# Top-k attention feeding a leaky-ReLU MLP on one core: eight small MLP chunks at the start instead of two, other units hurried, and eight units scored ahead instead of twelve

## The chip, the cores and the metric

The kernel runs on one core of one Trainium2 chip. The metric is the device time of one launch in microseconds (us). The kernel before takes 1465.96 us, the median of 3 runs (1465.23 to 1466.16). Work is done by five engines that run side by side: TensorE (PE in the profile, its weight loads PEld), VectorE (DVE), ScalarE (ACT), GpSimd (POOL) and SyncE (SP), which here issues the DMAs.

## The reference

Everything is float32 at the inputs and the output. There are 8 batches, 8 heads, 576 positions and a head width of 64.

```python
scores = scale * np.matmul(q, k.transpose(0, 1, 3, 2))
kth = np.partition(scores, -top_k, axis=-1)[..., -top_k:-top_k + 1]      # top_k = 32
scores = np.where(scores >= kth, scores, -1000000000.0)
scores = scores - np.max(scores, axis=-1, keepdims=True)
attn = np.exp(scores)
attn = attn / (np.sum(attn, axis=-1, keepdims=True) + 1e-09)
attn_out = np.matmul(attn, v)
x = attn_out.transpose(0, 2, 1, 3).reshape(4608, 512)
h = x @ w_in                          # 512 x 2048
out = np.maximum(0.01 * h, h) @ w_out # 2048 x 512
```

## The kernel before

**Units and steps.** The attention is cut into 144 units, one for each step of the main loop (line 609). A unit is 128 query rows of one pair of heads (or 64 rows of two pairs, where 576 isn't a multiple of 128). Four units in a row, one for each pair of heads, complete 128 tokens of the MLP's input `x`. A unit passes through the loop as `cur`, `old` and `older`: in step s, DVE finds the 32 largest scores of unit s (`top_k`, lines 289 to 306), POOL masks unit s-1 (lines 314 and 315), ACT takes its exponentials (line 318), and unit s-2 is normalised (lines 327 and 330) and transposed. The scores of two units are made on PE two steps ahead (`scores`, line 225), and copied out of PSUM by ACT (line 232).

**Transposing.** As a rule ACT splits the weights of a unit into 16-bit halves (line 339), SP writes them to DRAM (line 340), and a transposing DMA brings them back as `wT` (line 344). For units named in `HASTY` PE transposes them itself (`transpose_in_haste`, line 354, nine transposes), and ACT copies them to `wT` (line 360).

**Values.** `values_at(n)` says in which step, and where in it, PE multiplies a unit's weights with the values (`weigh_values`, line 381, two units at a time). Units below `UNHURRIED` (14) go to the middle of the step (n | 1) + 4, later ones to the end of the step (n | 1) + 3, and those in `HURRIED` one step sooner. ACT then copies the result to `x` (line 395).

**The MLP.** `CHUNKS` cuts the 4608 tokens into 2 chunks of 128 and 17 of 256. A chunk becomes ready when its last unit's values are in. A chunk of 256 tokens runs `w_in` as the stationary operand and `x` as the moving one (line 437), ACT applies the leaky ReLU (line 443), and PE multiplies with `w_out` (line 449). The first `EARLY` (2) chunks take another way, `hidden_of_few`: `x` is stationary, `w_in` moves 512 columns at a time (line 405), ACT applies the leaky ReLU into the tile `scale` (line 410), and PE transposes the result back (`turned`, line 421), which ACT copies to `gT` (line 422). In PSUM the tiles `ph`, `pt` and `pz` share the two buffers of the tag `ml`.

**The order on PE.** All engines run their instructions in the order in which the loop emits them. `mlp_steps(budget)` emits MLP work seven times in a step (`SLOTS`) until the budget, counted in matmul columns, is used up. The budget is a constant `EARLY_SHARE` (500) until the first chunk of 256 tokens is due, and after that the backlog spread evenly over the steps to the next due chunk. By the kernel's own count a chunk of 128 tokens of the early kind costs 17,408 columns and a chunk of 256 tokens 32,768.

**Units scored ahead.** The scores of twelve units named by `KEPT` (24, 25, 32, 33; 40, 41, 48, 49; 56, 57, 64, 65) are made in steps 0 to 5, while PE has no MLP work (`keep_scores`, line 276; how many in each step is in `EARLY_SCORES`). ACT copies them to `gT`, which the MLP doesn't use yet (line 280), SP writes them to DRAM (line 282), and they are fetched by DMA three steps ahead of their unit (line 287).

**Ahead of the loop.** The weights arrive as 64-bit words and are rounded on chip (`round_weights`); queries and keys for the units scored ahead are loaded into `raw` tiles by `load_early` (line 253).

Of the kernel before, what the change touches and what calls it, by code (L numbers as in the profile page):

```python
# [20 lines left out]
def kernel(  # L21
# [29 lines left out]
    WCH = 1024  # L51
    LEFT = S % P
    assert D == 64 and S == 576 and HP == 4 and B % 2 == 0 and LEFT == 64
    CHUNKS = [128] * 2 + [256] * 17
    assert sum(CHUNKS) == B * S
    CHMAX = max(CHUNKS)
    LOADED, LOADED_V = 5, 5
# [119 lines left out]
    def load_v(pi):  # L177
        v_of[pi] = loads.tile([P, NKC, 2, D], F32, name="vt", bufs=LOADED_V)
        nc.sync.dma_start(v_of[pi], vk[pi])
# [54 lines left out]
    def first_scores(u):  # L234

        ps = [ps_sc.tile([P, 2, 512], F32, name="wide", bufs=2) for i in range(2)]
        for half in range(2):
            for i, pi, side, r0 in u.parts:
                qt, kt = qk_of[pi]
                d = slice(side * D, (side + 1) * D)  # L240
                nc.tensor.matmul(ps[i][:, half, 0:HS], qt[d, u.q0:u.q0 + P],
                                 kt[d, half * HS:(half + 1) * HS], start=True, stop=True)
        yield
        u.both = work.tile([P, 2, S], F32, name="s_sb", bufs=5)
        u.s = [u.both[:, i, :] for i in range(2)]
        for i in range(2):
            nc.scalar.copy(u.s[i].rearrange("p (h n) -> p h n", h=2), ps[i][:, :, 0:HS])  # L247
# [109 lines left out]
    def keep_transposed(u):  # L357
        u.wT = work.tile([P, 2 * NKC - 1, P], F32, name="wT", bufs=3)
        for c0, c1, pt in u.parts_T:
            nc.scalar.copy(u.wT[:, c0:c1, :], pt[:, 0:c1 - c0, :])  # L360

    x_of = {}

    def x_at(token):

        c = 0
        while token >= CHUNKS[c]:
            token -= CHUNKS[c]  # L370
            c += 1
        return c, token
# [15 lines left out]
    def keep_values(u, po):  # L388
        n = u.rows
        po = po.rearrange("p (o n) -> p o n", n=n)  # L390
        ch, col = x_at(u.b * S + u.q0)
        if ch not in x_of:
            x_of[ch] = [xpool.tile([P, CHMAX], F32, name=f"x{c}") for c in range(HP)]
        for o, (pi, _, _) in enumerate(u.outs):
            nc.scalar.copy(x_of[ch][pi % HP][:, col:col + n], po[:, o, :])  # L395

    EARLY = 2

    def hidden_of_few(ch, x):

        g_of = {}
        for j in range(NFC // 4):
            ph = ps_ml.tile([P, 512], F32, name="ph", tag="ml")
            for c in range(HP):
                nc.tensor.matmul(ph, x[c][:, 0:P], w_in[c][:, j * 512:(j + 1) * 512],
                                 start=(c == 0), stop=(c == HP - 1))
                if c == 1:
                    yield 2 * 512
            g_of[j] = raws.tile([P, 2 * DMODEL], U16, name="scale", bufs=2).bitcast(F32)
            nc.scalar.activation(g_of[j], ph, AF.Prelu, alpha=SLOPE)  # L410
            yield 2 * 512
            if j:
                yield from turned(j - 1, g_of)
        few[ch] = g_of
# [3 lines left out]
    def turned(j, g_of):  # L418
        pt = ps_ml.tile([P, 4, P], F32, name="pt", tag="ml")
        for i in range(4):  # L420
            nc.tensor.transpose(pt[:, i, :], g_of[j][:, i * P:(i + 1) * P], ident)
        nc.scalar.copy(gT[:, 4 * j:4 * (j + 1), 0:P], pt)
        yield 2 * P

    def mlp(ch):

        n = CHUNKS[ch]
        t0 = sum(CHUNKS[:ch])
        x = x_of[ch]
        if ch < EARLY:  # L430
            yield from hidden_of_few(ch, x)
        for f0 in range(0, NFC if ch >= EARLY else 0, 2):
            ph = ps_ml.tile([P, 2, CHMAX], F32, name="ph", tag="ml")
            for i in range(2):
                f = f0 + i
                for c in range(HP):
                    nc.tensor.matmul(  # L437
                        ph[:, i, 0:n], w_in[c][:, f * P:(f + 1) * P], x[c][:, 0:n],
                        start=(c == 0), stop=(c == HP - 1),
                    )  # L440
                    if c == 1 or i == 0 and c == HP - 1:
                        yield 2 * max(n, 225)
            nc.scalar.activation(gT[:, f0:f0 + 2, 0:n], ph[:, :, 0:n], AF.Prelu, alpha=SLOPE)  # L443
            yield 2 * max(n, 225)
        for r0 in range(0, n, P):
            m = min(P, n - r0)
            pz = ps_ml.tile([P, 512], F32, name="pz", tag="ml")
            for f in range(NFC):
                nc.tensor.matmul(  # L449
                    pz[0:m, 0:DMODEL], gT[:, f, r0:r0 + m], w_out[f // 4][:, f % 4, :],  # L450
                    start=(f == 0), stop=(f == NFC - 1),
                )
                if f % 2 and f + 1 < NFC:
                    yield 2 * DMODEL
                if f == 7 and ch in few:
                    yield from turned(NFC // 4 - 1, few[ch])
            o_sb = work.tile([P, DMODEL], F32, name="o_sb", bufs=1)
            nc.scalar.copy(o_sb[0:m], pz[0:m, 0:DMODEL])  # L458
            nc.sync.dma_start(out[t0 + r0:t0 + r0 + m, :], o_sb[0:m])
            yield 2 * DMODEL  # L460

    def mlp_cost(ch):
        n = CHUNKS[ch]
        if ch < EARLY:
            return NFC * DMODEL + NFC // 4 * (HP * 512 + 2 * P)
# [21 lines left out]

    LAG = 3
    HURRY = 20
    HURRIED = (15, 23, 31)  # L490
    HASTY = (14, 15, 23, 31)
    UNHURRIED = 14
    MIDDLE, END = 0, 1

    def values_at(n):

        if n < UNHURRIED:
            return (n | 1) + LAG + 1, MIDDLE
        return (n | 1) + LAG - ((n | 1) in HURRIED), END

    steps = units

    KEPT = (24, 40, 56)
    EARLY_SCORES = {0: 4, 1: 2, 2: 1, 3: 2, 4: 1, 5: 2}

    def unit(n):
        return steps[n] if 0 <= n < len(steps) else None
# [2 lines left out]
    for n, u in enumerate(steps):  # L510
        ch, _ = x_at(u.b * S + u.q0)
# [11 lines left out]
    def slot_budget(s):  # L523

        after = [at for (at, _), _ in ready_at if at >= s]
        until = after[0] if after else s
        if len(after) >= len(CHUNKS) - EARLY:
            return EARLY_SHARE
        return backlog[0] / ((until + 1 - s) * SLOTS)

    EARLY_SHARE = 500
    SLOTS = 7

    with tc.manual_schedule():
        last = {p: n for n, u in enumerate(steps) for p in u.pairs}

        to_keep = [[steps[n] for n in (a, a + 1, a + 8, a + 9)] for a in KEPT]
        early_units = {u for us in to_keep for u in us}
        to_load, to_keep = list(to_keep), [u for us in to_keep for u in us]
# [27 lines left out]
        jobs = [round_weights(*job) for job in ROUNDED] if AS_WORDS else [iter(())] * len(ROUNDED)  # L567
        for n in range(len(jobs) + 1):
            if n == len(jobs) - 1:
                first = first_scores(steps[0])  # L570
                next(first, None)
            for job in jobs[max(n - 1, 0):n + 1][::-1]:
                next(job, None)
            if n == len(jobs) - 1:
                next(first, None)
                load_v(0)
                load_v(1)
            elif n == len(jobs):
                for _ in first_scores(steps[1]):
                    pass  # L580
            if n:
                load_weights(n + 2)
            if n >= len(jobs) - 2:
                load_early(to_load.pop(0))
            if 0 <= n - len(jobs) + HP + 1 < HP:
                load_qk(n - len(jobs) + HP + 1)

        def weights_of(u):
            reciprocals(u)
            normalize(u, 0)  # L590
            normalize(u, 1)
# [17 lines left out]
        for s in range(len(steps) + LAG + 1):  # L609
# [9 lines left out]

            at_first = s < HURRY and s - 2 in HURRIED  # L620
            if at_first:
                weights_of(older)
            slot()
            if old:
                mask(old, 0)
                mask(old, 1)
            late = s < HURRY and not {s - 1, s - 2} & set(HURRIED)
            if older and not late and not at_first:
                weights_of(older)
            mlp_steps(budget)  # L630
            weighed = values(s, MIDDLE)
            at_once = s - 2 in HASTY or any(at == (s, MIDDLE) for at, _ in ready_at)
            if at_once:
                keep(weighed, s, MIDDLE)
            slot()
            if older and late:
                weights_of(older)
            if s - 2 in HASTY:
                transpose_in_haste(older)
# [4 lines left out]
            if older:  # L644
                keep_transposed(older) if s - 2 in HASTY else transpose(older, lambda: mlp_steps(budget))
            if not older or s - 2 in HASTY:
                mlp_steps(budget)
# [18 lines left out]
            if new and s >= HURRY:  # L666
                scores(new)
            score_early(EARLY_SCORES.get(s, 0))
            budget = slot_budget(s + 1)
# [61 lines left out]
```

## Time and profile before

| | us |
|---|---|
| median of the runs (three) | 1465.96 |
| the profiled execution's own time | 1463.63 |
| its span, first to last instruction | 1461.7 |
| PE busy | 1405.5 |
| DVE busy | 1320.3 |
| ACT busy | 1100.9 |
| POOL busy | 1097.8 |
| step 0 begins on DVE | 61.4 |
| first MLP matmul on PE | 130.8 |
| step 43 begins on DVE | 449.2 |
| last `top_k` on DVE ends | 1375.7 |

All views are of the one profiled execution. A group row gives line, engine, operation, tiles, shapes and count, then the busy time in us and the mean duration in ns of one instruction, and after the second bar the idle time just ahead of these instructions and what ended it. A float32 matmul shows as two records, a transpose as one. Because matmuls overlap in the pipeline, the time that one record takes of PE is busy time divided by count, and not the mean duration. A row of the windows view gives a stretch of time, then the busy time of each engine in it, the granted clock of PE (1.00 is full) and the DMA share.

### The profile page before, as it was taken

To read this page: it belongs to the slowest core of one execution; us is meant where nothing else is said; L and a number is where in the kernel's file an instruction comes from. 1 tells how busy PE (TensorE), PEld (TensorE's weight loads), DVE (VectorE), ACT (ScalarE), POOL (GpSimd) and SP (SyncE) were. 2 spreads that over 40 slices of the span, in tenths; PEclk is the share of its full clock that TensorE was granted. 3 is DMA by queue.
4 is the path that set the end of the run, shared out by engine and by line. 5 is a ranking of instruction groups with operands and counts; after the bars stand their busy time and mean duration, and the time that the engine had idled before them with its cause. 6 is when DMAs were issued, how large, how long until landed. Compare 5 with 4: busy or idle time off the path is not lost.

```text
span 1461.7 us, 24213 instructions
## 1 busy us (share of the span) xinstructions
PE 1405.5 (96%) x8066; PEld 932.9 (64%) x8068; DVE 1320.3 (90%) x3401; ACT 1100.9 (75%) x1984; POOL 1097.8 (75%) x744
## 2 busy tenths in 40 slices
PE   7848999999989999999999999999999999999998
PEld 2425548576757676767676767676766666666674
DVE  7999999999999999999999999999999999999600
ACT  8878878677868777777778787777777777777710
POOL 3288888878888888888888787888887878787700
PEclk9968999999999999999999999999999999999999
DMA  8967543646576666676656655666566665554510
GB/s 320 344 219 225 140 119 101 194 128 181 151 192 179 172 167 188 156 194 169 157 163 170 169 138 141 171 164 166 149 156 171 164 151 143 153 141 130 150 43 14
DMA packets 394989, 239.03 MB, mean 164 GB/s; under 512 B 334576, under 2 KB 336112, under 8 KB 392944
## 3 DMA queue, kind: packets, MB, share of 16 engines
q1 hardware_dynamic: 394864, 237.48, 58.5%
q8 instruction: 63, 1.03, 0.3%
q14 instruction: 62, 0.51, 0.1%
HBM read 55.77 MB, written 99.09 MB: 106 GB/s over the span
## 4 chain that ended last, share of the span: by engine, by line
PE 77%; DVE 13%; ACT 4%; DMA 4%; issue 1%; SPq 0%; POOL 0%; DVEq 0%; ACTq 0%; POOLq 0%
PE pz L449 30%; PE ph L437 29%; PE wide L381 10%; DVE tops L301 5%; PE wide L225 5%; DVE pairs L304 4%; PE narrow L225 3%; DMA apart<-split 2%; ACT split L339 1%; DVE pairs L296 1%; DMA raw<-in_weights_dram 1%; ACT s_sb L318 1%; ACT s_sb L330 1%; DVE w_out L156 1%; DMA wT<-apart 1%
## 5 line engine op out<-in xcount | busy, mean ns | idle before, releaser
L314 POOL TENSOR_SCALAR pen<-s_sb,tops 128x576 f32<-128x576 f32 x288 | 638.3, 2216 | 203.8 <-DVE tops L301 135.6
L301 DVE MAX8 tops<-pairs 128x8 f32<-128x288 f32 (+1 forms) x1152 | 635.9, 591 | 0.0
L449 PE MATMUL pz<-w_out,gT 128*128 128x512 f32 x1152 | 505.1, 595 | 2.4 <-ACT scale L410 2.4
L437 PE MATMUL ph<-x,w_in 128*128 128x256 f32 x2176 | 482.6, 381 | 0.0
L304 DVE MATCH_REPLACE8 pairs<-tops,pairs 128x288 f32<-128x288 f32 (+1 forms) x864 | 460.1, 538 | 0.0
L437 PEld LDWEIGHTS ph<-x,w_in 128*128 128x128 f32 x2176 | 409.5, 190 | 75.5 <-issue 21.3
L315 POOL TENSOR_TENSOR s_sb<-s_sb,pen 128x576 f32<-128x576 f32 x288 | 406.9, 1413 | 24.0
L449 PEld LDWEIGHTS pz<-w_out,gT 128*128 128x128 f32 x1152 | 216.4, 190 | 266.2 <-issue 261.2
L339 ACT COPY split<-s_sb 128x1152 uint16<-128x1152 uint16 x280 | 309.5, 1146 | 1.7 <-DMA apart<-split 1.7
L330 ACT ACTIVATE s_sb<-s_sb,rz 128x576 f32<-128x576 f32 x288 | 207.7, 773 | 33.4 <-DVE rz L327 33.4
L318 ACT ACTIVATE s_sb<-s_sb,nbias 128x576 f32<-128x576 f32 x288 | 222.4, 772 | 6.4 <-POOL s_sb L315 6.4
L296 DVE TENSOR_TENSOR pairs<-s_sb 128x576 f32<-128x576 f32 x288 | 213.6, 780 | 9.5
L381 PEld LDWEIGHTS wide<-wT,vt 128*64 128x64 f32 x3200 | 161.2, 139 | 53.0 <-issue 36.2
L381 PE MATMUL wide<-wT,vt 128*64 128x128 f32 (+1 forms) x3200 | 179.0, 268 | 10.3 <-DMA wT<-apart 4.7
L443 ACT ACTIVATE gT<-ph 128x512 f32<-128x512 f32 x136 | 80.7, 593 | 58.6 <-PE ph L437 57.7
L395 ACT COPY x<-wide 128x128 f32<-128x128 f32 (+1 forms) x160 | 32.2, 260 | 120.2 <-PE wide L381 120.2
L232 ACT COPY s_sb<-wide 128x704 f32<-128x704 f32 x130 | 98.0, 754 | 20.1 <-PE wide L225 20.1
L458 ACT COPY o_sb<-pz 128x512 f32<-128x512 f32 x36 | 21.1, 585 | 92.3 <-PE pz L449 92.2
L225 PE MATMUL wide<-kt,qt 64*128 64x352 f32 (+1 forms) x360 | 70.4, 507 | 1.0 <-ACT s_sb L247 0.7
L232 ACT COPY s_sb<-narrow 128x448 f32<-128x448 f32 x130 | 62.9, 536 | 1.2 <-PE narrow L225 0.6
L304 DVE MATCH_VALUE_LOAD pairs<-tops,pairs 128x8 f32 x864 | 62.6, 72 | 0.0
L327 DVE RECIPROCAL rz<-ze 128x2 f32<-128x2 f32 x144 | 22.3, 155 | 42.3 <-ACT ze L323 42.1
(67 smaller groups left out, 678.0 us busy)
## 6 DMA issues: line engine op xcount, KB each, us to landing
apart<-split SPq DMA_DIRECT2D x280, 288.0 KB, 2.1
raw<-in_weights_dram SPq DMA_DIRECT2D x15, 1024.0 KB, 6.9
vt<-in_vk_dram SPq DMA_DIRECT2D x32, 320.0 KB, 3.7
out_dram<-o_sb SPq DMA_DIRECT2D x36, 256.0 KB, 2.8
kept<-gT SPq DMA_DIRECT2D x12, 576.0 KB, 3.2
s_sb<-kept SPq DMA_DIRECT2D x12, 576.0 KB, 4.8
qt<-in_qT_dram SPq DMA_DIRECT2D x20, 288.0 KB, 3.5
kt<-in_kT_dram SPq DMA_DIRECT2D x20, 288.0 KB, 3.4
```

The source lines that it names most:

```text
L225: nc.tensor.matmul(to[r0:r0 + u.rows, i, :], qt[d, u.q0:u.q0 + u.rows], kt[d, k0:k1], start=True, stop=True)
L296: nc.vector.tensor_tensor(pairs[:, :, n, :], u.both[:, :, 0:HS], u.both[:, :, HS:S], op)
L301: nc.vector.max(out=u.tops[:, i, r, :], in_=rest[i])
L304: nc.vector.match_replace(out=rest[i], in_to_replace=u.tops[:, i, r, :], in_values=rest[i], imm_value=LOWEST)
L314: nc.gpsimd.tensor_scalar(pen, u.s[i], u.tops[:, i, ROUNDS - 1, 7:8], MASKED, ALU.is_lt, ALU.mult)
L315: nc.gpsimd.tensor_tensor(u.s[i], u.s[i], pen, ALU.add)
L318: nc.scalar.activation(u.s[i], u.s[i], AF.Exp, bias=u.nbias[:, i:i + 1], scale=SCALE, accum_out=u.z[:, i:i + 1])
L330: nc.scalar.activation(u.s[i], u.s[i], AF.Copy, bias=0.0, scale=u.rz[:, i:i + 1])
L339: nc.scalar.copy(split, pairs[:, :, h])
L381: nc.tensor.matmul(po[side * D:(side + 1) * D, o, :], vt[:, c, side, :], u.wT[:, c + side * NKC if c + 1 < NKC else c, r:r + n], start=(c ...
L437: nc.tensor.matmul(ph[:, i, 0:n], w_in[c][:, f * P:(f + 1) * P], x[c][:, 0:n], start=(c == 0), stop=(c == HP - 1),)
L449: nc.tensor.matmul(pz[0:m, 0:DMODEL], gT[:, f, r0:r0 + m], w_out[f // 4][:, f % 4, :], start=(f == 0), stop=(f == NFC - 1),)
```

## The change

Eight chunks of 128 tokens (`CHUNKS`, `EARLY = 8`) come ahead of 14 of 256. All units' values now come at the end of step (n | 1) + 3 (`UNHURRIED = 0`), one step sooner for units 2, 3, 6, 7, 38, 39, 46 and 47 (`HURRIED`), of which 2, 3, 6, 7, 39 and 47 are transposed on PE (`HASTY`). Eight units instead of twelve are scored ahead (72, 73, 80, 81, 96, 97, 104 and 105), five in step 0 and three in step 1. `EARLY_SHARE` goes from 500 to 550 and now holds until the ninth chunk is due. The set `read` and the assertions act while the program is built and emit nothing.

```diff
-    CHUNKS = [128] * 2 + [256] * 17
+    CHUNKS = [128] * 8 + [256] * 14
...
-    x_of = {}
+    x_of, read = {}, set()
...
         if ch not in x_of:
+            assert ch < 2 or ch - 2 in read
             x_of[ch] = [xpool.tile([P, CHMAX], F32, name=f"x{c}") for c in range(HP)]
...
-    EARLY = 2
+    EARLY = 8
...
         if ch < EARLY:
             yield from hidden_of_few(ch, x)
+            read.add(ch)
...
-    HURRIED = (15, 23, 31)
-    HASTY = (14, 15, 23, 31)
-    UNHURRIED = 14
+    HURRIED = (3, 7, 39, 47)
+    HASTY = (2, 3, 6, 7, 39, 47)
+    UNHURRIED = 0
...
-    KEPT = (24, 40, 56)
-    EARLY_SCORES = {0: 4, 1: 2, 2: 1, 3: 2, 4: 1, 5: 2}
+    KEPT = (72, 96)
+    EARLY_SCORES = {0: 5, 1: 3}
...
-    EARLY_SHARE = 500
+    EARLY_SHARE = 550
...
-            if n >= len(jobs) - 2:
+            if n >= len(jobs) - 2 and to_load:
                 load_early(to_load.pop(0))
```

More of the change, by code (lines that the diff above doesn't have):

```diff
@@ L444, in mlp @@
             yield 2 * max(n, 225)
+        read.add(ch)
         for r0 in range(0, n, P):
```

## The prediction

> **What bounds the kernel now.** I read the slices of the page first, then the windows view cut at the moments that matter, then the chain.
>
> ```profile
> PE   7848999999989999999999999999999999999998
> ...
> DVE  7999999999999999999999999999999999999600
> ...
> PEclk9968999999999999999999999999999999999999
> ```
>
> One digit is 36.5 us. PE has holes only in the first four slices, and only there is its clock lowered. DVE ends two slices ahead of PE.
>
> ```profile
> 61.40:130.80 69.40, 41.66 (x243) 27.33 (x241) 68.88 (x182) 52.20 (x94) 52.59 (x36) 0.73 0.72 238
> 130.80:222.60 91.80, 87.82 (x492) 46.63 (x490) 89.18 (x233) 75.89 (x145) 75.48 (x51) 0.98 0.53 141
> 222.60:449.20 226.60, 219.40 (x1303) 150.28 (x1305) 220.36 (x575) 171.85 (x323) 187.16 (x126) 0.99 0.59 160
> 449.20:1375.80 926.60, 926.27 (x5574) 638.78 (x5571) 892.24 (x2324) 729.79 (x1339) 756.74 (x506) 1.00 0.60 160
> 1375.80:1462.00 86.20, 82.08 (x324) 50.02 (x322) 0.35 (x3) 17.25 (x31) 6.79 (x4) 1.00 0.18 50
> ```
>
> The first figure after a window is its length, the next PE's busy time, the third DVE's. From 61.4 us (step 0) to 130.8 (the first MLP matmul) DVE works without a gap, and PE lacks 28 us. From 130.8 to 449.2 the two are close: a step lasts about 8.85 us where DVE alone sets it (step starts in the DVE timeline 61.4, 70.1, 78.9), and PE lacks 4.0 and 7.2 us. From 449.2 on PE lacks 0.3 us in 926 and sets the pace.
>
> ```profile
> 1402.59 27.82 PE ph L437 x128
> 1430.42 27.48 PE pz L449 x64
> ```
>
> The end of the chain of waits (start, length, what) is one whole chunk on PE. So the kernel is **PE's work from the first MLP matmul on**: the last matmul ends at 1457.9, thus 1327.1 us after 130.8, of which 1315.6 are busy (the sum of the last four windows) and 11.5 idle. What the change does is counted in four terms: when that work begins, how much it is, how much idle time is in it, and at what clock it runs.
>
> **What the Trainium skill says.** "TensorE: Matmul & The Clock Gate", section "What's actually happening", says that PE's clock is halved after an idle window of some 3.4 us and restored after a busy one. The trace agrees: 0.73 between 61.4 and 130.8, 1.00 later. "PSUM — Partial Sum Buffer", section "Engine vs sequencer instructions", says that ScalarE works strictly in order and that matmuls start in program order, so a late `wT` or a late leaky ReLU stops everything behind it on PE. The trace agrees (below). "Trainium Kernel Development and Optimization", Best Practices, warns that matmul busy time is a poor measure of distance from the peak; I use busy time only as a price of work, and never infer headroom from it.
>
> **The start, -13.8 us.** Before, chunk 0 waits for units 2 and 3 in the middle of step 7 (123.2 us). Now it is the end of step 5, which begins on DVE at 105.4. The chain there, from rows of before: unit 3's mask on POOL starts at 96.7 and takes 2 x (2.2 + 1.4) us, to 104; exponential and sums on ACT to 105.2; in step 4 ACT also has the score copies of units 6 and 7 (2.6 us) and the `x` copies of units 0 and 1, so normalising (2 x 0.77) ends near 110.5; nine transposes on PE (0.155 each) near 112; the copies to `wT` (1.2) and the values of two units (2.4) near 115.5; `x` copies and the first matmul near **117** (115 to 119). Nothing earlier is delayed by the five and three units scored in steps 0 and 1: before, the four of step 0 end on ACT at 72.0 and the two of step 1 at 81.6, and unit 0 is normalised at 83.6; one unit more costs ACT 1.3 us in each step. DVE has to wait at the head of steps 5 and 9 for the sums of units 3 and 7, some tenths of a us.
>
> **The work, +22.8 us.** Six more half chunks take the way of the few.
>
> ```profile
> L449 PE MATMUL pz<-w_out,gT 128*128 128x512 f32 x1152 | 505.1, 595 | 2.4 <-ACT scale L410 2.4
> L437 PE MATMUL ph<-x,w_in 128*128 128x256 f32 x2176 | 482.6, 381 | 0.0
> ...
> L405 PE MATMUL ph<-w_in,x 128*128 128x512 f32 x64 | 29.4, 602 | 1.2 <-ACT scale L410 1.2
> ...
> L421 PE MATMUL pt<-ident,scale 128*128 128x128 f32 x32 | 5.0, 278 | 0.0
> ```
>
> Busy by count: 438 ns a record of line 449, 222 of line 437, 459 of line 405, 155 of line 421. 128 tokens cost 64 x 222 = 14.2 us in a chunk of 256, or 32 x 459 + 16 x 155 = 17.2 in one of the few; the 14.0 us of line 449 are common. The 459 contain the ends of short runs (a run of 12 took 437 each), so the difference lies between 2.5 and 3.0; 2.7 x 6 = **+16.2**. Scores of units 8 and 9 now lie behind the first MLP matmul: 2.14 us for a pair in the timeline, **+2.2**. Four kept units fewer, each 1.1 us of line 225 in the loop: **+4.4**; that their 2.9 us of line 276 leave steps 2 to 5 gains nothing, for there PE idles. Transposes on PE behind the start are four units' worth in both kernels. ACT gets 4 x 0.59 us more for each of the six half chunks, 14 us in 36 steps of 8.85 in which it is under 85% busy: hidden, unless PE waits for it (next). DMA loses the round trips of four early units and four kept ones; nothing on PE waited for bandwidth there, so I take nothing. The queue and key loads for pairs 5 to 7 move from step 5 to step 1 on SP, behind the last kept writes; the first `wT` of unit 0 is then needed only in step 4, so nothing is added. PSUM's two `ml` buffers and the two `x` buffers are not over-asked: chunk 6's hidden part is emitted in step 35, a step ahead of the first write for chunk 8.
>
> **Idle time, -5.0 us.** With 550 columns in seven slots, a step holds 3,850 of 17,408 columns of 31.2 us, thus 6.9 us, and some 2.3 of attention (18.4 us in eight steps: 73.8 less 55.4 for a chunk, the last two chain lines), together 9.2 against 8.85 on DVE: PE falls behind at once and becomes the bound from step 6 on, as it is after 449.2. So the waits of before, which came where DVE was the slower, should mostly go. They are: 4.25 us at 427 for a late `wT`, 1.7 at 270, 1.1 at 222, and behind late leaky ReLUs
>
> ```profile
> 188.19 3.70 PE L405 MATMUL ph<-w_in,x 128*128 128x512 f32 x8 [0.86 <-ACT scale L410]
> ...
> 194.47 2.42 PE L449 MATMUL pz<-w_out,gT 128*128 128x512 f32 x4 [2.14 <-ACT scale L410]
> ```
>
> (the bracket is the idle time ahead and what ended it). Even an ACT that is free leaves some 0.25 us there (the wait at 151.7), because only four transposes cover the leaky ReLU. I take 0.5 us for each of eight chunks, 2.5 for the first steps until PE lags: 6.5 instead of 11.5. Neither the waits of six more such chunks nor those of `wT` in steps 8 to 14 at the earlier place are in the trace: from 0.2 to 3.0 us for a chunk (the second chunk of before), so 1.5 to 25 in all.
>
> **Clock, -2.0 us.** Two windows of 3.4 us at half speed behind 195.9 and 431.4 follow the waits above and cost 1.7 each; I keep 1.4 for a cold start at 117.
>
> **Sum**: -13.8 + 16.2 + 2.2 + 4.4 - 5.0 - 2.0 = +2.0 us, so 1465.6 against the profiled 1463.63. The runs' median is 2.3 above the profiled one: **1468.0**. 0.2% of this kernel, 2.9 us, is about what a measurement can tell from no change.
>
> **Rivals.**
> A, the sum above, own range -3 to +7 us (1463 to 1473); chance 0.42.
> B, **faster**: PE is as full from step 6 on as it is after 449 (idle 1.5), starts at 115, pays 2.5 a chunk, and no clock loss stays: -15.8 + 15 + 2.2 + 4.4 - 10 - 3.4 = -7.6, with the start at 117 about -6: 1460. For it: 0.3 us idle in 926. Against: those chunks have 3.5 us of cover for each leaky ReLU, these 0.6. Chance 0.33.
> C, **slower**, leaky ReLU on ACT: each of the eight chunks loses what the two of before lost on average (0.38, 0.25, 0.08, 0.86 and 2.14 over two: 1.86), 15 us in place of 11.5, the clock as before: -13.8 + 16.2 + 2.2 + 4.4 + 3.5 = +12.5, or 1478.5. It decides from about 1.3 us a chunk (10 us idle, +5.5). For it: ACT goes up in just these steps. Against: when PE lags, ACT has its other work done. Chance 0.17.
> D, the promise isn't kept: the `x` of chunk 0 stands behind ACT's other work, or `wT` comes late in steps 8 to 14, and the start or a later step slips by 4 to 8 us: 1472 to 1476. Chance 0.08.
>
> **From this to the numbers.** Faster by over 0.2% is nearly all of B and the low edge of A, 0.37; within, most of A, 0.25; slower the upper part of A, C and D, 0.38. The range runs from B's -8 to just beyond C.
>
> **What would show it.** Right: the first matmul of line 406 (405 before) near 117 us; PE busy some 10 us higher (1415), since four kept units leave line 276 (-11.6), lines 225 (+4.4), the few (+16.2) and two units' transposes (+2.8) grow, and clock loss goes (-2); PE idle behind the start near 6.5; step 59 on DVE, when both kernels have the chunks of the first 1536 tokens behind them, at about 601 (before 592.9), for no unit up to there has its scores from DRAM now (10 x 1.1 = 11 us of line 225 more), and 6.6 us of that won back by step 106, where eight units have them instead of two. Wrong: a start beyond 121, waits of line 406 or 452 for `scale` above 10 us in all, or DVE still at 8.85 us a step between steps 10 and 40.

## The result: the changed kernel is half a per cent slower

The changed kernel takes 1473.54 us, the median of 4 runs (1471.82 to 1474.67), beside 1465.6 for the kernel before on the same chip: a ratio of 1.0054, 95% interval 1.0036 to 1.0071, or some 7.9 us. The profiled execution took 1472.42 us, its span 1470.3.

The windows view of the changed kernel, cut like that of before (length, PE busy, PEld, DVE, ACT, POOL, PE's clock, DMA share, GB/s):

```profile
61.80:117.90 56.10, 31.03 (x212) 21.85 (x210) 55.65 (x146) 38.88 (x73) 41.29 (x28) 0.76 0.58 197
117.90:222.60 104.70, 100.01 (x524) 52.72 (x522) 98.16 (x259) 81.67 (x156) 83.39 (x56) 1.00 0.37 102
222.60:459.50 236.90, 231.21 (x1285) 126.37 (x1281) 225.35 (x586) 191.72 (x359) 190.68 (x129) 1.00 0.56 152
...
459.50:1383.60 924.10, 920.08 (x5512) 632.61 (x5511) 890.68 (x2322) 726.32 (x1335) 756.27 (x505) 1.00 0.61 160
...
1383.60:1470.30 86.70, 83.09 (x326) 50.52 (x324) 1.36 (x4) 18.26 (x33) 7.24 (x4) 0.99 0.20 53
```

The first MLP matmul starts at 117.95 us instead of 130.8, and PE's last one ends at 1466.7 instead of 1457.9. Of the 1348.7 us between, 1334.3 are busy and 14.4 idle. The same count for before was 1315.6 and 11.5. So the 8.8 us between the two ends are **-12.9 for the start, +18.8 of work and +2.9 of idle time**. The row that surprises is the fourth: behind step 43, where PE lacked 0.3 us in 926, it now lacks 4.0 in 924.

The groups of PE by shape, where the work went (busy, then mean ns of one):

```profile
L452 PE MATMUL pz<-w_out,gT 128*128 128x512 f32 x1152 | 506.6, 595 | 1.8 <-ACT scale L411 1.8
L439 PE MATMUL ph<-x,w_in 128*128 128x256 f32 x1792 | 397.5, 381 | 0.0
...
L406 PE MATMUL ph<-w_in,x 128*128 128x512 f32 x256 | 116.8, 601 | 6.0 <-ACT scale L411 6.0
...
L422 PE MATMUL pt<-ident,scale 128*128 128x128 f32 x128 | 19.4, 274 | 0.0
```

Line 406 (405 before) grew by 87.4 us and line 422 by 14.4, and line 439 (437) lost 85.1: 16.7 us more for six chunks, 2.8 each. Last, who keeps PE waiting behind the start, from the waits views of 117 to 460 us

```profile
PE ph L406 <- ACT scale L411: 6.0, 13, 1.2
PE pz L452 <- ACT scale L411: 1.8, 7, 0.3
PE wide L354 <- ACT s_sb L330: 1.3, 1, 1.3
```

and from 459.5 us to the end (total us, times, longest):

```profile
PE wide L381 <- DMA wT<-apart: 2.8, 5, 1.1
PE wide L381 <- DMA vt<-in_vk_dram: 1.2, 2, 0.7
```

The leaky ReLU costs 7.8 us in 20 short waits, about 1 us a chunk. In before it was 3.6, with late values, late transposed weights and one wait for `wT` copies making 7.5 more; of these the changed kernel has 0.8 up to step 43 and 4.0 behind it.

### The profile page after: what moved, and what is told of

It is laid out like the page before. It is cut to its first block, busy times and chain, and to the rows that moved or that the text cites. A ratio compares the mean times of both kernels' runs of the same rounds, so it can differ in the third digit from the quotient of the medians.

```text
span 1470.3 us, 24024 instructions
## 1 busy us (share of the span) xinstructions
PE 1413.8 (96%) x7988; PEld 904.0 (61%) x7990; DVE 1320.4 (90%) x3401; ACT 1110.7 (76%) x2008; POOL 1097.9 (75%) x744
## 4 chain that ended last, share of the span: by engine, by line
PE 79%; DVE 9%; ACT 5%; DMA 5%; issue 1%; SPq 0%; POOL 0%; DVEq 0%; ACTq 0%; POOLq 0%
PE pz L452 31%; PE ph L439 24%; PE wide L381 10%; PE wide L225 5%; PE ph L406 5%; DVE tops L301 3%; PE narrow L225 3%; DVE pairs L304 3%; DMA wT<-apart 2%; ACT split L339 2%; DMA raw<-in_weights_dram 2%; ACT s_sb L318 1%; DVE pairs L296 1%; DMA vt<-in_vk_dram 1%; ACT scale L411 1%
## 5 line engine op out<-in xcount | busy, mean ns | idle before, releaser
L439 PE MATMUL ph<-x,w_in 128*128 128x256 f32 x1792 | 397.5, 381 | 0.0
L439 PEld LDWEIGHTS ph<-x,w_in 128*128 128x128 f32 x1792 | 337.2, 190 | 61.7 <-issue 17.2
L339 ACT COPY split<-s_sb 128x1152 uint16<-128x1152 uint16 x276 | 305.8, 1147 | 0.7 <-DMA apart<-split 0.5
L406 PE MATMUL ph<-w_in,x 128*128 128x512 f32 x256 | 116.8, 601 | 6.0 <-ACT scale L411 6.0
L232 ACT COPY s_sb<-wide 128x704 f32<-128x704 f32 x134 | 101.1, 755 | 23.1 <-PE wide L225 23.1
L445 ACT ACTIVATE gT<-ph 128x512 f32<-128x512 f32 x112 | 66.5, 593 | 52.3 <-PE ph L439 51.8
L406 PEld LDWEIGHTS ph<-w_in,x 128*128 128x128 f32 x256 | 46.7, 190 | 61.9 <-issue 51.8
```

Of the source, the lines that this page charges most:

```text
L339: nc.scalar.copy(split, pairs[:, :, h])
L439: nc.tensor.matmul(ph[:, i, 0:n], w_in[c][:, f * P:(f + 1) * P], x[c][:, 0:n], start=(c == 0), stop=(c == HP - 1),)
```

## The experiments

Each of the twelve was timed against the kernel before on its own chip (1465.6 to 1466.4 us in the four groups of runs; ratios are taken within a group). For each, the count from its profiled execution: where the first MLP matmul starts, PE busy and idle from there to its last matmul, and the stretches at half clock that begin in between, in brackets the part of them in which PE works. Half of that part is lost, and stands in the busy time; in the stretches of 10 us and more PE is idle for 4 to 9 us.

| kernel | us | ratio to before, 95% | start | busy | idle | half clock (PE at work) |
|---|---|---|---|---|---|---|
| before | 1465.6 | 1 | 130.8 | 1315.6 | 11.5 | 6.8 (6.6) |
| changed | 1473.5 | 1.0054 (1.0036 to 1.0071) | 117.9 | 1334.3 | 14.4 | 0 |
| two small chunks | 1481.6 | 1.0103 (1.0086 to 1.0120) | 118.3 | 1325.3 | 34.1 | 27.3 (12.1) |
| four | 1480.1 | 1.0096 (1.0082 to 1.0110) | 116.5 | 1329.7 | 28.0 | 17.1 (9.9) |
| four, share 500 | 1474.6 | 1.0056 (1.0043 to 1.0069) | 116.9 | 1328.6 | 23.8 | 13.7 (8.5) |
| six, share 535 | 1476.0 | 1.0063 (1.0051 to 1.0076) | 116.2 | 1332.1 | 21.9 | 13.7 (8.0) |
| twelve kept | 1478.7 | 1.0091 (1.0077 to 1.0104) | 122.9 | 1332.9 | 16.3 | 6.8 (6.1) |
| kept sooner | 1480.7 | 1.0095 (1.0082 to 1.0109) | 116.4 | 1337.5 | 20.9 | 6.8 (6.8) |
| transposes amid matmuls | 1471.1 | 1.0038 (1.0025 to 1.0051) | 116.2 | 1334.1 | 18.2 | 3.4 (3.4) |
| transposes twice | 1477.2 | 1.0071 (1.0057 to 1.0085) | 116.1 | 1346.4 | 9.6 | 3.4 (3.4) |
| unhurried start | 1481.6 | 1.0101 (1.0086 to 1.0117) | 130.3 | 1333.7 | 16.9 | 10.2 (8.9) |
| before, four small | 1477.0 | 1.0066 (1.0052 to 1.0080) | 132.0 | 1322.6 | 15.6 | 10.2 (8.7) |
| before, amid matmuls | 1465.7 | 0.9995 (0.9987 to 1.0003) | 131.3 | 1314.2 | 13.9 | 3.4 (3.3) |
| before, kept later | 1471.8 | 1.0032 (1.0020 to 1.0044) | 131.6 | 1316.6 | 16.6 | 10.2 (5.9) |

Start, busy and idle add up to the end by definition. What the runs tell is how each term answers to an edit. The changed kernel and the seven runs that keep its early start begin between 116.1 and 118.3 us, so a single profile is no surer than some 2 us.

**Fewer small chunks, with the early start kept.**

```diff
-    CHUNKS = [128] * 8 + [256] * 14
+    CHUNKS = [128] * 2 + [256] * 17
...
-    EARLY = 8
+    EARLY = 2
```

> The changed kernel with the chunks as before (2 of 128 tokens by the way of the few, 17 of 256), all else changed. Theory T (from the first MLP matmul on PE is the bound, and the six more chunks of the few cost it some 2.8 us of work and 1 us of waiting for the leaky ReLU each, more than the early start gains): PE loses 17 us of work and 6 of waits, but then DVE sets the pace up to step 42 (36 steps of 8.87 us = 319 against 313 of PE's work), so the gain is cut to 9 to 13 us: about 1462 us, step 43 on DVE near 448 instead of 459.5. Rival K (the cost is in the other edits, above all four units fewer scored ahead and the values half a step to a step sooner): 1470 to 1477, as the changed kernel. Rival S (the early start is what is lost when only two chunks are small, because PE then starves between steps 15 and 18): slower than the changed kernel, 1478 or more.

The same edit with 4 and 16:

> The changed kernel with four chunks of 128 tokens by the way of the few and 16 of 256. Theory T: four times 3.8 us less for PE, 15 us, of which DVE's pace leaves some 10: about 1463 us, and no starving. Rival K: 1470 to 1477. Rival S: better than with two small chunks by some 5 us or more.

Theory T fell: 8 us slower with two and 7 with four, where 11 faster was expected. Rival K's 1470 to 1477 fell too. Rival S had it right for two, and its guess for four (5 us better than two) was too high. The waits view of the run with two, 119 to 460 us:

```profile
PE wide L381 <- ACT s_sb L232: 22.4, 3, 11.2
```

PE has nothing left to do between its small chunks and the first chunk of 256 tokens (due at the end of step 18 here). Its clock is halved for 24 us from 210 to 241 us, but PE works in only 8.7 of them, so some 4.4 us are lost by it. With four, the hole lies at steps 24 to 26 and ends with the transposed weights (117 to 460 us):

```profile
PE wide L381 <- DMA wT<-apart: 14.7, 4, 8.8
```

I had argued that DVE sets the pace up to step 42 anyway, so that such holes cost nothing. They cost everything: step 43 begins at 460.8 and 459.7, no sooner than in the changed kernel (459.5), and the backlog is paid behind it. With two, PE works 15.0 us less up to step 43 and is idle 15.8 us more; behind step 43 it works 5.9 us more and is idle 3.9 us more.

**The share matched to the chunks.**

```diff
-    EARLY_SHARE = 550
+    EARLY_SHARE = 500
```

with four chunks;

> Four chunks of 128 tokens as in the run with four, but the share at 500 instead of 550, the share that the kernel before has. Theory F (PE must be fed, and no faster than it can be: end = start + work + idle + time lost at half clock; with share 550 the four chunks are done by step 22 and PE then starves until the first chunk of 256 comes at the end of step 26): 4 x 17,408 columns in 20 steps need 3,480 a step, 500 x 7 gives them, so idle behind the start falls from 28 to some 16 us, the cold clock of 17 us from step 24 to 28 goes, and the work is four times 2.8 us less than in the changed kernel: 118 + 1323 + 16 + 2, about 1464 us, step 26 to 30 without waits for transposed weights over 3 us. Rival N (the share only moves the idle time, because DVE sets the pace of these steps in either case): 1477 to 1482, as with four and 550.

and 535 with six:

> Six chunks of 128 tokens and 15 of 256, share 535 (6 x 17,408 columns in the 28 steps until the first chunk of 256 at the end of step 34 need 3,730 a step, 533 x 7). Theory F: 28 steps of PE's work are 6 x 31.2 + 28 x 2.3 = 252 us against 248 of DVE's, so PE is just fed; two chunks' 2.8 us and 1 us of waits less than in the changed kernel: about 1466 us (1463 to 1469). Rival N or one in which the small chunks don't matter: 1471 to 1476.

Theory F's figures fell by some 10 us in both. With four chunks 500 is 5.5 us better than 550, so rival N falls for that pair; with six its 1471 to 1476 came true. Idle time with four is 23.8 us and not 16: the hole is smaller, and stays (one wait of 7.1 us for `wT` at step 26, and one of 8.1 with six at step 34), and behind step 43 there are 7.5 us. Neither beats eight chunks. So from the early start on, every count tried from two to eight ends at 1473 to 1482: fewer chunks pay in idle time and clock what they save in work.

**The start alone.**

```diff
-    HURRIED = (3, 7, 39, 47)
-    HASTY = (2, 3, 6, 7, 39, 47)
+    HURRIED = (39, 47)
+    HASTY = (39, 47)
```

> The changed kernel without the hurry for units 2, 3, 6 and 7 (chunk 0 comes at the end of step 6, and units 2, 3, 6, 7 are transposed by DMA). Theory F: the first MLP matmul comes one step later, +8.9 us (near 127), two units' transposes (2.8 us) and the wait ahead of them (1.4) leave the time behind the start: 4 to 6 us slower, about 1478.5. Rival V: no slower than 1474.5.

Some 8 us slower than the changed kernel, with the first MLP matmul at 130.3. Rival V falls. The profiled execution is the slowest of its four (1486.5 us): its start is 12.4 us later, its work about the same (1333.7, some 4.5 of it lost at half clock) and its idle time 2.5 us longer, 14 us in all, so the table's row overstates the loss. The early start, with the transposes on PE that it takes, is worth some 8 us, and it is the part of the change that gains.

**The price of a small chunk alone**, on the kernel before, whose start stays:

```diff
-    CHUNKS = [128] * 2 + [256] * 17
+    CHUNKS = [128] * 4 + [256] * 16
...
-    EARLY = 2
+    EARLY = 4
```

> The kernel before with four chunks of 128 tokens by the way of the few instead of two, all else as before (same start of the MLP near 131 us). It prices the small chunk without the early start. Theory G: 2 x 2.8 us of work and 2 x 1 us of waits, of which 2 to 3 fill idle time: 4 to 6 us slower, about 1470.5. Rival C (a small chunk costs twice that, since ACT is short of time): 1474 or more. Rival V (hidden behind DVE): 1465 to 1467.

10.6 us slower for two chunks. Between the profiled executions it is 12.3: 7.0 of work (about 1 of it half clock), 4.1 of idle time, 1.2 of start. Rival C's figure, but not its reason: the waits for the leaky ReLU grew only from 3.6 to 5.1 us; 2.5 of the idle time are `wT` waits behind step 43, where before had none.

**The wait for the leaky ReLU.** In `hidden_of_few`:

```diff
                 if c == 1:
                     yield 2 * 512
+                    if j:
+                        yield from turned(j - 1, g_of)
...
             yield 2 * 512
-            if j:
-                yield from turned(j - 1, g_of)
```

> The changed kernel with the transposes back of block j-1 emitted in the middle of the hidden matmuls of block j instead of behind them, so that each leaky ReLU has some 1.8 us of matmuls as cover instead of 0.6; the same instructions. Theory T: of the 7.8 us in which PE waits for lines 411 some 1.5 are left, and as PE is the bound there, 6 us go: about 1467.5, with the waits of line 406 and 454 for scale at 1 to 2 us. Rival A (ACT is short of time in these steps, so that the wait comes back at the next instruction that needs ACT, or the lead of DVE is what counts): less than 2 us, 1471.5 or more.

The median gained 2.5 us, between the two forecasts, and the intervals overlap. Waits for `scale` are gone, and others stand in their place: PE now waits 4.6 us for the copies to `gT` (line 423), which free the buffers that the next block needs. The profiled run, the slowest of its five, is 5.2 us ahead at step 59 (601.4 us instead of 606.6), of which 1.7 are its earlier start, and has lost the lead by step 107 (1042.2 and 1041.5); its `wT` waits behind step 43 are 7.0 us instead of 2.8. On the kernel before:

> The kernel before with the transposes back emitted in the middle of the next block's hidden matmuls, as in the run on the changed kernel. Theory G (end = start + work + idle, idle being what each edit leaves or takes): of the 3.6 us in which PE waits for the leaky ReLU some 1.5 are left, 2 us faster than before: about 1463.5. Rival V (DVE sets the pace between 130 and 450 us in this kernel, so a wait of PE there costs nothing): 1465 to 1467.

No difference, in 13 runs. Leaky ReLU or copy waits stay at 3.4 us, and `wT` waits grow from 4.7 to 6.8 up to step 43. Rival V is right here in what it says of the time.

**The transposes doubled.**

```diff
-        for i in range(4):
+        for i in (0, 1, 2, 3) * 2:
             nc.tensor.transpose(pt[:, i, :], g_of[j][:, i * P:(i + 1) * P], ident)
```

> The changed kernel with each transpose back of the hidden activations (line 422) done twice: 128 more transposes of 0.152 us, 19.5 us on PE. Theory F (PE is the bound in the steps of the small chunks, whatever DVE does): 17 to 21 us slower than the changed kernel, about 1493. Rival V (DVE is the bound in steps 6 to 41, PE's work there is partly hidden): less than 10 us slower, below 1484.

Only 3.6 us slower than the changed kernel, with overlapping intervals. Rival V's figure came true, but not its reason: between its first MLP matmul and step 43 PE is idle for only 4.0 us, so DVE doesn't hide the work. Theory F's price was wrong in two ways. By shape, the transposes in this run:

```profile
L422 PE MATMUL pt<-ident,scale 128*128 128x128 f32 x256 | 33.4, 273 | 0.0
```

That is 14.0 us for 128 more, 0.11 each and not 0.152. And the waits view (115 to 470 us):

```profile
PE ph L406 <- ACT scale L411: 1.5, 4, 0.7
```

They fell from 7.8 to 1.5 us: the added transposes run while PE would have waited. In a small chunk, transposing back and the wait for the leaky ReLU are one stretch of time, and its length is set by the leaky ReLU as much as by the transposes.

**The units scored ahead.** Twelve in the changed kernel:

```diff
-    KEPT = (72, 96)
-    EARLY_SCORES = {0: 5, 1: 3}
+    KEPT = (72, 96, 112)
+    EARLY_SCORES = {0: 5, 1: 3, 2: 1, 3: 1, 4: 1, 5: 1}
```

> The changed kernel with twelve units scored ahead (112, 113, 120, 121 too, one in each of the steps 2 to 5). Theory T: four times 1.1 us less of scores where PE is the bound: 4.4 us, about 1469. Rival K: at least 6 us faster, below 1467.5. Rival D (the fetches from DRAM crowd the DMAs and make the transposed weights late, as the waits between 580 and 1030 us hint): no gain, 1472 or more.

5 us slower instead of 4 faster. The unit scored in step 5 runs on PE from 121.1 to 122.9 us, just ahead of the first MLP matmul. The copies of the one of step 4 stand on ACT ahead of unit 3's weights, which are normalised from 114.2 us instead of 110.7. So the start slips by 5 us. Work fell by 1.4 us net of 3.0 lost at half clock, so the 4.4 are there and were overtaken. Rival K falls. Rival D's figure came true, but waits behind step 43 grew by only 2.2 us (6.2 instead of 4.0). Then the same eight sooner:

```diff
-    KEPT = (72, 96)
+    KEPT = (24, 40)
```

> The changed kernel with its eight units scored ahead taken sooner (24, 25, 32, 33, 40, 41, 48, 49). Theory D (the waits of PE for vt and wT behind step 43, 4.0 us here and 0.3 before, come from the fetches in steps 70 to 105): they go to below 1.5 us, while the scores saved count the same in steps 22 to 48, where PE is the bound too: about 1470. Rival W (those waits come with the new order of the chunks, not with the fetches): no gain, 1473 or more, and more if DVE sets the pace in steps 22 to 48.

7 us slower, and theory D falls: of the 4.0 us of waits for `vt` and `wT` behind step 43, 3.5 remain, and up to step 43 there are now 4.7 us for `wT` and 3.1 for `vt` instead of 0.8. As many scores are left out of the loop as in the changed kernel, and the half clock after such waits (6.8 us, 3.4 lost) accounts for the 3.2 us by which its work grew. Rival W is nearer, though its reason for the loss (DVE's pace) isn't what the waits show. And twelve later in the kernel before:

```diff
-    KEPT = (24, 40, 56)
+    KEPT = (56, 72, 96)
```

> The kernel before with its twelve units scored ahead taken later (56, 57, 64, 65, 72, 73, 80, 81, 96, 97, 104, 105 in place of 24 to 65). Theory G: the eight units that are now scored in the loop between steps 22 and 48 give PE 8.8 us of work, of which some 4 fill the idle time at 222, 270 and 427 us, and the same 8.8 us leave the stretch where PE has no idle time: 4 us faster, about 1462. Rival D (fetches from DRAM and loads stand in one queue on SP, and units fetched late make values or transposed weights late near step 95, as in the runs with four and six chunks): 1466 or more, with PE waits for vt or wT of 2 us or more near 935 us.

Rival D is right: 5.4 us slower, with its wait of 2.0 us for `vt` at 934 us. The largest wait it did not name. Idle time up to step 43 fell from 11.2 to 4.6 us as theory G had it, but behind it rose from 0.3 to 12. The waits view from 449 us on:

```profile
PE narrow L225 <- DMA kt<-in_kT_dram: 6.5, 1, 6.5
PE wide L381 <- DMA wT<-apart: 2.4, 3, 1.5
PE wide L381 <- DMA vt<-in_vk_dram: 2.0, 1, 2.0
```

And SP's timeline there, with what each instruction issues:

```profile
701.11 0.52 SPq L287 DMA_DIRECT2D s_sb<-kept  x1
...
710.25 0.52 SPq L287 DMA_DIRECT2D s_sb<-kept  x1
...
719.15 0.58 SPq L651 DMA_DIRECT2D qt<-in_qT_dram  x1
...
726.94 0.58 SPq L651 DMA_DIRECT2D kt<-in_kT_dram  x1
```

In each step the code issues either a fetch or the next query or key load (`if ... fetch_scores ... elif waiting`). Two fetches push the keys back by two steps (in the kernel before, `qt` is issued at 699.1 and `kt` at 707.4 us), and PE, in order, waits for them from 724.1 to 730.6 us.

## Why the prediction was right, and which term was not

Its forecast was +2 us, 1468.0, with a range of 1458 to 1480. The 1473.5 found are 5.5 us above the forecast and just beyond the own range of case A (1463 to 1473), towards C; it is the width of the whole range, from B to C, that took them in. Start and work came out nearly as reckoned, and the idle time did not; 2.0 us less of work than forecast hid a part of that, which is luck.

PE's rows of the start in the changed kernel:

```profile
111.53 1.43 PE L354 MATMUL wide<-ident,s_sb 128*128 128x128 f32 x9 [1.21 <-ACT s_sb L330]
113.95 4.07 PE L381 MATMUL wide<-wT,vt 128*64 128x128 f32 x40 [0.99 <-ACT wT L360]
117.95 0.70 PE L406 MATMUL ph<-w_in,x 128*128 128x512 f32 x1
```

- **Start**: -13.8 forecast, -12.9 found. The chain ran as written: nine transposes of unit 3 at 111.5 us, the values from 113.95; these took 4.1 us at half clock instead of 2.4. The unhurried run confirms the term.
- **Work and clock**: +22.8 and -2.0 forecast, together +20.8; +18.8 found. The half clock of before (6.8 us, 3.4 lost) went altogether: it followed waits of 2.1 and 4.2 us, and the longest wait behind the start is now 1.35. A small chunk costs 2.8 us by the rows, 2.7 forecast; line 225 grew by 5.0 against 6.6.
- **Idle time**: the term that was mis-sized. 6.5 us forecast, 14.4 found, so +2.9 where -5.0 stood: 7.9 of difference. Three parts: leaky ReLU 7.8 us (0.5 a chunk was taken, 1.0 found); 1.3 ahead of unit 6's transposes; 4.0 behind step 43, taken as zero.
- The step behind it, that PE lags from step 6 on and that a PE which sets the pace doesn't wait, failed in its second half. PE did lag (from step 6 to 43 a step took 9.3 us on average, DVE no longer at 8.85), but of the 32 leaky ReLUs of the eight chunks 20 made PE wait, 0.25 us or more each, the last in step 40. With eight transposes as cover instead of four (the run with transposes twice) 4 did.
- Step 59 came at 606.6 us (601 forecast), and 5.8 us of the 13.7 behind before came back by step 107 (6.6 forecast): PE works 7.8 us less between the two steps than before, and idles 2.0 us more. So the eight kept units save what was said. PE busy was 1413.8 (1415 forecast). B's premise, PE as full as after 449 us, is not met even there.
- "DMA: I take nothing" was too bold. Fetches share SP's order with the loads; in the kernel before with late fetches this is shown. For the 4.0 us of the changed kernel it isn't shown: four of its seven waits (1.6 us, in steps 56, 58 and 135) lie where nothing is fetched, with fetches moved sooner 3.5 us remained, and with two small chunks it is 7.8. So neither the late fetches nor the eight chunks account for them alone; what sets them stays open.

So the change trades 12.9 us of earlier start for six chunks whose way costs 2.8 us each in work and about 1 us in waits, and for 4.4 us of scores back in the loop. No half of it could be had alone in these runs: without the chunks PE starves, without the hurry 8 us are lost. None beat the kernel before.

## What to carry to other kernels

When one engine is busy to the end, write its end as start plus work plus idle, and ask of each edit which term it moves and whether another answers; here starting sooner needed smaller chunks to be fed, and these cost more. An idle hole early in the run isn't free because another engine sets the pace at that time: the work it didn't do is still there at the end. Before a DMA is moved to a better time, look at what it displaces in the queue that issues it.

## What the runs showed of the hardware

- Transposes on PE cost less back to back than a group's mean tells: a group of four takes 0.60 us, one of eight 1.04, so the next ones cost 0.11 us each.
- Waits of PE of 6.5 to 11 us went with 10 to 14 us of half clock at a time. These stretches began 2 to 5 us into the wait and outlasted it by 4 to 6 us; half of that, 2 to 3 us, is what each cost in addition to the wait. After a shorter wait the half clock can come late: in the kernel before, a wait that ended at 194.5 us was followed by 3.4 us of it from 195.9.
- The stretches are multiples of 3.4 us, the window that the Trainium skill names in "TensorE: Matmul & The Clock Gate", section "What's actually happening".
